# A new written order for a fused attention and two-layer kernel, with fewer changes of array division

## The chip, the core and the metric

The kernel runs on one core of a Trainium2 chip. A core has five engines, each with its own list of instructions that it takes strictly in turn: TensorE (PE), which multiplies matrices on an array of 128 by 128 cells and writes to the accumulation memory (PSUM); VectorE (DVE) and ScalarE (ACT), which work element by element and carry results out of PSUM; GpSimd (POOL) and SyncE (SP), which here mostly issue transfers (DMAs). Engines wait for one another through semaphores that the framework puts in where data or buffers pass between them. The metric is the device time of one execution in microseconds (us); less is better.

The array can be divided. A product of 128x128 uses all of it. Products of 64x64 use quarters, four of them side by side. Transposes on the array use a third division (112x64 or 128x64 here).

## The reference

Inputs are q, k and v (8 batches, 12 heads, 448 positions, 64 per head) and two weight matrices, all float32. The output is 3584 rows of 768, float32.

```python
scores = scale * np.matmul(q, k.transpose(0, 1, 3, 2))     # scale = 1/8
attn = np.maximum(scores, 0.0) ** 2 / S                    # S = 448
attn_out = np.matmul(attn, v)
x = attn_out.transpose(0, 2, 1, 3).reshape(B * S, H * D)   # 3584 x 768
h = x @ w_in                                               # 2048 wide
g = 0.5 * h * (1.0 + erf(h * inv_sqrt2))
out = g @ w_out                                            # 768 wide
```

## The kernel before

Everything is computed in bfloat16 with float32 accumulation. Heads are taken in three groups of four per batch. For batches 0 and 1, q and k are transposed on the array (`add_tq`, `add_tk`, lines 605 and 633) and copied out by ACT or DVE. For batches 2 to 7 they are transposed by transfers, nine per batch, issued by SP (`add_T_dma`, line 660; called turns below: for each group one of k and two of q).

A score piece (`add_steps`, line 734, tile `ps`) is four 64x64 products of 448 columns, one per quarter of the array, into one of three score banks (pool `w_pp`). ACT or DVE then applies the relu (lines 746 and 748) and DVE squares (line 755). After seven score pieces a group's product with v follows (`add_av`, line 795, tile `pav`, 28 products, also in a score bank), and two copies carry it to the transposed x (`xT`, lines 511 and 513). Batch 0 does all of this in halves of 224 columns.

The first layer takes, for batches 0 to 4, pieces of six 128x128 products of 448 columns (`add_f1`, line 847, tile `psh`), each followed by a gelu on ACT (line 857). Batches 5 to 7 use seven products for four blocks (`add_block`, line 991, tile `pb`) with sums on DVE. The second layer works on groups of 256 rows: group 0 plainly (`add_plain`, line 1277), groups 1 to 13 with seven products of eight matmuls each instead of eight (`add_group`, line 1166, tile `pso`). Their evictions are sums on DVE (line 1200) or copies, and SP stores the rows (line 1125).

In the last group the products are, by entry: P1407, P1409, P1411, P1413, then P1415 and P1416 (one product cut into 256 and 128 columns), P1419 (384 columns), and P1421 and P1422 (again 256 and 128). D1406 is the sum that P1421 and P1422 read. D1414 follows P1413, D1417 P1415, D1418 P1416, D1420 P1419, D1423 P1421 and D1424 P1422. S1425 to S1428 store: S1426 all 768 columns of 128 rows as a 48 KB and a 336 KB transfer, S1427 256 columns and S1428 128 columns of the other 128 rows, these two issued half by ACT and half by SP.

What comes when is written out by hand. The kernel first makes 1432 steps (`Op`), each with a function that issues its instructions. The string `ORDER` lists them all: a letter for the engine (P for PE, A for ACT, D for DVE, G for POOL, S for SP) and the step's number; Z is a filling product of zeros on PE. `place` walks through this list, `run` then calls the functions in that order, and so the order of every engine's own list, and which engine takes a relu or a copy, is what the string says:

```python
        for word in ORDER.split():
            if word[0] == "Z":
                op, eng = next(fills), "PE"
            else:
                op, eng = self.open[int(word[1:])], names[word[0]]
...
        for _, op, eng in self.log:
            op.fn(eng)
```

Since the list is complete, the costs and due times that the scheduler class also holds choose nothing; they only fill its own clock. On POOL the loads of batch b+2 stand behind gates (`add_gate`, line 701), one for each group, small copies that wait until the turns of batch b+1 have been read out of the buffers that the loads will overwrite. On SP the stores stand in one line with the turns, and a store that waits for its rows holds the turns behind it.

Before all that, PE runs warm products of zeros, 128x128 by 512 columns, while the first q and k arrive:

```python
    for _ in range(SPIN):
        nc.tensor.matmul(spin[:, 0, :], zero, zeros, start=True, stop=True)
```

Of the kernel before, what the change touches and what calls it, by code (L numbers as in the profile page):

```python
# [79 lines left out]
SPIN = 10  # L80
# [3 lines left out]
G3 G1 G0 G4 G7 G1431 G2 A10 P11 D13 A16 G6 P17 D12 P14 D18 G118 P42 P39 P21 D15 P23 G5 A43 P36  # L84
D22 P33 G117 A40 P19 D24 P25 D44 G121 A34 D20 G9 Z480 P54 P48 D41 A37 P51 D26 Z448 D38 A55 P63
P27 P29 A49 D52 P57 D28 P81 A64 D35 P69 P31 D53 G122 A58 P45 D30 D65 A82 P75 G8 D50 P131 D32 A70
P66 D59 A76 P93 D56 D46 A67 P60 D77 D47 A94 P84 P108 D71 P129 A61 G120 D68 A62 P78 D95 A109 P72
D130 D132 A79 P105 G123 D73 A85 P111 A74 D80 P96 G119 P143 D110 A106 D112 P90 D83 A97 P102 P165
D86 A144 G124 P141 A91 D166 P171 P87 A103 D98 A142 P156 D92 P133 D107 A172 P99 D104 A157 D113
P114 A88 G125 A100 D89 P135 A101 G126 A115 P168 P159 D116 G128 P174 A134 P251 A136 D169 D158  # L90
P180 A175 P145 D173 A160 A252 D181 P195 P162 P192 A146 D182 P243 D170 A193 G154 P253 D163 A196
G147 D176 A244 P198 G148 P189 D167 P186 A254 P137 D164 G151 P139 D161 A190 G150 P177 D138 A187
D140 P213 A199 P247 D178 A179 P207 P210 D214 G127 P245 A248 D200 G153 A208 P265 G149 A211 A246
P204 P216 P183 S228 P263 A205 D217 A266 P219 S229 P222 D194 P249 A264 D188 A223 S230 P257 D184
A250 D224 P259 D206 A220 D209 A258 P267 D197 D212 A260 D215 P255 D218 A268 S234 D221 P225 D185
A256 D191 S235 P201 A226 S232 P282 D227 P276 P261 A202 S233 D203 A283 P350 A262 S231 P358 A351
P348 S236 A359 P360 A277 G240 A349 G238 P354 G239 A361 P352 A355 G237 G241 P285 P288 P306 A353
P356 G155 D286 P364 G271 D307 A357 G242 G272 P318 P294 D289 P374 A365 P362 D295 A375 D319 P303
P291 D287 P279 A363 P370 D320 D278 A292 P378 A280 D304 A371 G274 D293 P309 P330 P312 D305 A379
P366 D284 D296 P372 D281 A367 P376 D313 A310 D290 G270 A331 P315 P300 G152 A373 P297 A377 D301  # L100
P368 D314 D332 A316 P333 D311 P324 P382 G269 A369 D317 G275 A334 D390 G273 D302 D419 P380 D383
D417 D418 P384 D308 A381 D393 A298 S399 D391 A325 D394 P336 S400 P387 D392 A337 A299 D338 D395
P327 P339 D385 P321 S386 A388 S398 D397 A340 P342 D396 P421 A322 S401 D328 A343 P423 D335 A422
D341 S403 P425 D323 D344 D424 P427 G407 D420 S402 D426 P429 D329 D428 S404 P443 P455 P446 D430
P433 S405 G410 D326 A444 D445 A447 P452 S406 P345 D562 A453 D456 P437 P440 D434 S436 P431 D346
A438 D347 G413 P513 G408 A441 D432 G412 P470 D457 P449 G409 P476 D442 A514 P509 G415 A450 D471
G414 P464 P479 P511 A510 G411 G416 A477 D465 P461 P494 D451 P515 A512 D448 D439 A495 P517 D454
A480 S543 P473 A462 P458 A518 A516 S541 D474 P467 P488 D481 P519 D472 S542 D560 P521 D459 A520
P523 A468 A522 P527 A489 A460 P503 A524 P500 P485 S549 A528 P525 A486 D501 P529 S546 D475 A526
D478 P497 D469 S547 P533 A530 D463 D490 P535 S435 D496 A534 S389 D466 P531 S544 A504 D498 P603  # L110
D505 P482 S548 A532 A536 D604 P491 P609 S545 P539 D561 A492 D563 P537 D502 A540 D483 P564 G556
D605 G558 A610 D499 A538 G550 D487 G557 P600 P615 D493 P566 A565 G551 D611 A601 G553 D484 G555
P612 P506 A616 G552 G554 D613 P606 P618 G559 D567 P568 D507 A508 P570 D607 A569 D608 S704 D617
P624 A619 P636 P630 P572 D620 D614 A637 D571 P574 A625 D602 D582 A631 D573 P627 P642 P651 D575
P576 A628 D643 A652 P633 D580 P639 P621 D577 S579 D626 A634 S706 D644 P666 P584 D581 S707 D632
P586 D640 A585 S578 D622 P588 A667 S705 D635 D587 D623 P590 S710 D638 D629 P663 P648 D641 S708
P645 G713 A649 D664 S711 P660 A589 P654 D665 P592 D583 A661 S709 D591 P594 D646 A655 D593 S712
D656 P657 P596 D650 D595 G716 A658 G718 D725 P676 A647 D662 G715 D668 P778 G719 D597 P769 G720
P766 A677 P678 G721 A779 D770 G714 P672 D780 A767 G717 A679 D659 P772 D653 P763 P669 A764 D773
P781 A673 P775 D765 P680 S869 A776 D782 P674 S599 D783 A681 S868 D771 P790 P682 D777 A675 D670  # L120
S598 A791 D774 P688 D768 A683 D671 P793 P787 P784 A689 S871 A788 D794 P805 P796 D792 S867 P684
D789 P686 S872 S870 G876 G878 G722 D785 A786 D806 A797 P811 D807 P802 A685 P799 P690 D798 A687
A803 D812 P692 A691 S873 D800 P694 G877 D801 A693 S875 D795 P700 D723 A695 D804 P814 P817 D724
P808 A815 D818 A701 P823 P820 D813 P698 D726 P696 D824 A699 D819 S874 P702 A697 D821 A809 P727
D825 A703 A810 P829 P912 P826 A728 P729 A830 D827 P921 A913 P924 D822 G882 P906 G883 P731 D828
A922 G879 D816 G881 D730 P733 G884 D923 D831 G880 D732 P832 D907 P918 G885 P735 D833 A919 D734
P737 A834 D908 D736 A925 D743 P933 P936 P915 D926 P739 A937 D934 D744 P942 A916 P909 P930 D738
P747 D740 S742 A910 S980 D943 P749 D917 A748 S979 P751 D931 D911 S978 D745 P948 P954 D750 P945
P753 A752 D914 S984 D746 A946 P755 D949 S983 D920 P957 P927 D950 S982 D754 D932 A958 P939 D756
P757 S985 D886 A940 D928 P759 S986 D941 A955 D938 D758 P960 P966 S761 P835 D959 S981 D760 A961  # L130
D929 P837 D887 S741 A836 D944 P839 S762 A967 D935 D947 P963 P969 D956 P951 A840 A970 D964 P972
A838 P990 D968 P843 D962 D888 A991 P841 A844 D973 P847 D952 A842 D974 A953 P845 D965 D971 A848
P987 P1002 P975 A846 A988 D1003 P993 P996 P849 D1004 A976 D992 P853 D997 A850 P859 D994 A854
D889 A977 P999 P1005 D1067 P1014 A860 P851 A1006 P855 D1015 A1000 D998 A852 D1007 P1029 P1023
D1001 P1011 A856 P857 D989 A1030 P863 D1012 A1024 D995 P1047 P1026 D1063 P1008 A864 A1048 D1027
P1041 A858 P1017 P861 D1028 A1009 D1068 A1018 D1010 P890 D1031 A862 D1059 P1053 A1042 P1020
P1050 D891 P865 D1013 A1021 D1019 P894 D1022 A1054 D1025 A1051 P1035 D1016 P1038 A866 P1032
D1060 A1039 D1043 P1044 P892 D1062 A1033 D1034 A1045 P1071 D1070 P1088 D893 P896 D1036 A1089
A895 D1049 P1073 A1072 D1179 P1090 D1069 P1079 D1040 P1092 D1055 P1096 D1074 D1052 P1077 P898
# [255 lines left out]
def kernel(  # L395
# [952 lines left out]
    zeros = zero[:, :1].to_broadcast([128, NB])  # L1348
    for _ in range(SPIN):
        nc.tensor.matmul(spin[:, 0, :], zero, zeros, start=True, stop=True)  # L1350
# [202 lines left out]
```

## Time and profile before

| | us |
|---|---|
| median of 3 runs | 371.25 (371.02 to 371.29) |
| the profiled execution's own time | 370.67 |
| its span, first to last instruction | 368.9 |
| PE busy with products | 359.5 |
| PE busy with weight loads, beside them | 218.2 |
| DVE busy | 295.6 |
| ACT busy | 187.9 |
| POOL busy | 62.6 |

The profile names a line by engine, operation and tile: `PE ps L734` is a score product, `PE psh L847` a first-layer product, `DVE a_sq L755` a square. A PE product counts as busy until its modelled end, and the products overlap, so busy time on PE is no proof that it is not waiting; the start of one product against the start of the next shows that better. The granted clock of the array is 0.998 of full pace over the span.

### The profile page before, as it was taken

The numbers are of one execution on the slowest core, as the hardware profiler recorded it, in microseconds if no ns is written. First come the engines' busy times: TensorE is split into PE (matmuls) and PEld (weight loads), VectorE is DVE, ScalarE is ACT, GpSimd is POOL, SyncE is SP. The second block draws the span as 40 slices with busy tenths as digits, with TensorE's granted clock in tenths as the row PEclk, the third lists the DMA queues.
The fourth block names the chain that finished last, engine by engine and source line by source line (L and its number), as shares of the span: only waits on it lengthen the run. The fifth ranks groups of instructions, "written<-read, shape, count | busy, mean of one in ns | idle before, by whom it ended". The sixth has DMA issues, their size and how long they took to land.

```text
span 368.9 us, 8397 instructions
## 1 busy us (share of the span) xinstructions
PE 359.5 (97%) x3532; PEld 218.2 (59%) x3532; DVE 295.6 (80%) x493; ACT 187.9 (51%) x300; POOL 62.6 (17%) x103
## 2 busy tenths in 40 slices
PE   8799999999999999999999999999999999999994
PEld 4566554455544455544555554477988778876663
DVE  3998671989884989999979998999976587677662
ACT  4999865554377565466445566861434113314200
POOL 8576206230050060022204000000000000000000
PEclk9999999999999999999999999999999999999999
DMA  9999999999989999989997994000200230022233
GB/s 171 199 201 204 201 176 157 204 201 196 191 147 188 204 129 190 211 96 196 205 145 108 205 168 133 0 2 2 87 0 3 85 87 3 12 75 85 87 86 85
DMA packets 89541, 47.26 MB, mean 128 GB/s; under 512 B 55328, under 2 KB 86048, under 8 KB 89504
## 3 DMA queue, kind: packets, MB, share of 16 engines
q0 software_dynamic: 32912, 22.47, 42.4%
q1 hardware_dynamic: 55952, 23.76, 34.4%
q8 instruction: 27, 0.44, 0.5%
q10 hardware_dynamic: 640, 0.51, 0.4%
q14 instruction: 10, 0.08, 0.1%
HBM read 45.61 MB, written 11.01 MB: 154 GB/s over the span
## 4 chain that ended last, share of the span: by engine, by line
PE 94%; DVE 3%; DMA 1%; ACT 1%; issue 0%
PE pso L1166 32%; PE psh L847 26%; PE pb L991 13%; PE ps L734 10%; PE pav L795 9%; PE pso L1277 3%; DVE a_sq L755 1%; DMA q<-in_q_dram 1%; ACT a_sq L746 1%; PE tp L605 1%; DVE qT L511 0%; PE tp L633 0%; DVE a_sq L748 0%; DVE osb L1200 0%; ACT nq L513 0%
## 5 line engine op out<-in xcount | busy, mean ns | idle before, releaser
L746 ACT ACTIVATE a_sq<-ps 128x896 bf16<-128x896 f32 (+1 forms) x114 | 100.2, 921 | 29.9 <-PE ps L734 29.7
L755 DVE TENSOR_TENSOR a_sq<-a_sq 128x896 bf16<-128x896 bf16 (+1 forms) x169 | 96.8, 615 | 1.2 <-ACT a_sq L746 0.8
L847 PE MATMUL psh<-xT,win_sb 128*128 128x448 bf16 (+1 forms) x516 | 97.3, 340 | 0.0
L748 DVE TENSOR_SCALAR a_sq<-ps 128x896 bf16<-128x896 f32 (+1 forms) x55 | 58.9, 1078 | 24.7 <-PE ps L734 24.6
L847 PEld LDWEIGHTS <-win_sb 128*128 128x128 bf16 x516 | 47.6, 98 | 46.1 <-issue 11.3
L857 ACT ACTIVATE h_sb<-psh 128x448 bf16<-128x448 f32 x80 | 43.3, 549 | 33.7 <-PE psh L847 33.5
L1166 PEld LDWEIGHTS <-s_sb 128*128 128x128 bf16 x432 | 40.7, 98 | 27.0 <-issue 3.6
L734 PE MATMUL ps<-qT,kT 64*64 64x448 bf16 (+1 forms) x756 | 48.7, 337 | 1.1 <-ACT a_sq L746 1.1
L1166 PEld LDWEIGHTS <-h_sb 128*128 128x128 bf16 x312 | 29.9, 98 | 20.2 <-issue 2.3
L1028 DVE TENSOR_TENSOR part<-pb,part 128x448 f32<-128x448 f32 x60 | 35.6, 619 | 7.4 <-PE pb L991 5.5
L1166 PE MATMUL pso<-wout_sb,h_sb 128*128 128x384 bf16 x208 | 38.1, 326 | 0.0
L1166 PE MATMUL pso<-wout_sb,s_sb 128*128 128x384 bf16 (+1 forms) x208 | 37.7, 324 | 0.1
L1166 PE MATMUL pso<-t_sb,s_sb 128*128 128x384 bf16 (+1 forms) x208 | 37.7, 324 | 0.0
L795 PE MATMUL pav<-a_sq,v_sb 64*64 64x448 bf16 (+1 forms) x756 | 36.3, 329 | 1.3 <-DVE xT L511 0.9
L734 PEld LDWEIGHTS <-kT 64*64 64x64 bf16 x756 | 18.6, 105 | 24.7 <-issue 19.9
L1200 DVE TENSOR_TENSOR osb<-pso,p_sb 128x384 f32<-128x384 f32 x39 | 21.6, 554 | 12.1 <-PE pso L1166 8.7
L1037 ACT ACTIVATE h_sb<-part 128x448 bf16<-128x448 f32 x36 | 18.6, 571 | 21.2 <-DVE part L1028 12.7
L991 PEld LDWEIGHTS <-win_sb 128*128 128x128 bf16 x288 | 27.6, 98 | 2.5 <-issue 0.4
L795 PEld LDWEIGHTS <-v_sb 64*64 64x64 bf16 x756 | 21.1, 107 | 12.6 <-issue 2.6
L701 POOL COPY gate<-qT 128x16 bf16<-128x16 bf16 x15 | 3.7, 247 | 111.5 <-DMA qT<-nq 111.5
L991 PEld LDWEIGHTS <-ws 128*128 128x128 bf16 x216 | 20.8, 98 | 1.1
L1200 DVE TENSOR_TENSOR osb<-pso,osb 128x384 f32<-128x384 f32 (+1 forms) x26 | 14.1, 544 | 7.8 <-PE pso L1166 7.5
(64 smaller groups left out, 299.8 us busy)
## 6 DMA issues: line engine op xcount, KB each, us to landing
nk<-in_k_dram POOLq DMA_DIRECT2D x23, 224.0 KB, 7.6
nq<-in_q_dram POOLq DMA_DIRECT2D x21, 224.0 KB, 7.0
v_sb<-in_v_dram POOLq DMA_DIRECT2D x5, 672.0 KB, 11.6
out_dram<-osb SPq DMA_DIRECT2D x8, 336.0 KB, 3.3
v_sb<-in_v_dram POOLq DMA_DIRECT2D x9, 224.0 KB, 8.2
out_dram<-osb SPq DMA_DIRECT2D x7, 288.0 KB, 3.2
out_dram<-osb SPq DMA_DIRECT2D x8, 240.0 KB, 3.2
win_sb<-in_moe_w_in_dram POOLq DMA_DIRECT2D x8, 192.0 KB, 9.4
```

What stands on the lines that cost most here:

```text
L734: nc.tensor.matmul(ps[64 * j : 64 * j + 64, e, x * w : x * w + w], kT[r, g, i * 128 + 64 * j : i * 128 + 64 * j + 64], moving, start=True, ...
L746: A.activation(ar, ps, AF.Relu, scale=c_att)
L748: V.tensor_scalar(ar, ps, c_att, 0.0, op0=mybir.AluOpType.mult, op1=mybir.AluOpType.max,)
L755: V.tensor_mul(box["a2"][:, :, :used], ar, ar)
L795: nc.tensor.matmul(pav[0][o2 : o2 + 64, e, :w], vt[b][r, 2 * g + e, bass.ts(i, D)], box["a2"][r, y, o : o + w], start=(i == 0), stop=(i == ...
L847: nc.tensor.matmul(ph[:, x * n : x * n + n], win_sb[:, kd, bass.ts(m + x, 128)], xT[b][:, kd, c], start=(kd == 0), stop=(kd == KD - 1),)
L857: A.activation(h_ring()[:, m : m + nm, o + c.start : o + c.stop], box[0][:, :S].rearrange("p (x n) -> p x n", x=nm), AF.Gelu,)
L991: nc.tensor.matmul(bank[name][:, y, z * HS : z * HS + HS], w[:, k, bass.ts(mm, 128)], right()[:, k], start=first and k == 0 and z == 0, st ...
L1028: V.tensor_add(get(to), ps(name), get(other))
L1037: A.activation(h_ring()[:, m : m + 2, o + half[c].start : o + half[c].stop], src().rearrange("p (x n) -> p x n", x=2), AF.Gelu,)
L1166: nc.tensor.matmul(box[bank][:, n0:n1], left()[:, kf], right()[:, kf, n0:n1], start=bool(need) and kf == 0, stop=kf == K2 - 1, skip_group_ ...
L1200: V.tensor_add(out()[:, n0:n1], box[bank][:, n0:n1], other()[:, n0:n1])
```

## The change

Two things change: the number of warm products goes from ten to nine, and the string `ORDER` is replaced. The steps are the same 1432, with two fills of zeros as before (the number behind Z is the width: the second has 480 columns instead of 448). Each engine's list is put in another order: PE's pieces, the evictions on ACT and DVE, the loads and gates on POOL, the turns and stores on SP. Some evictions also change engine: 34 relus go from ACT to DVE and 33 back, 13 copies of x go to DVE and 15 back, and of the second layer's evictions seven go to DVE and three back. In all ACT has 293 entries after 298, DVE 495 after 490. In the last group the piece of 384 columns moves ahead of the pieces of 128 and 256, and the last piece is now the one of 128 columns. The diff, cut to its first and last lines and to those with the turns and stores of batches 5 to 7:

```diff
@@ -77,89 +77,89 @@
 
 COLD_END = 0.0
 K_CUT = 4
-SPIN = 10
+SPIN = 9
 
 
 ORDER = """
-G3 G1 G0 G4 G7 G1431 G2 A10 P11 D13 A16 G6 P17 D12 P14 D18 G118 P42 P39 P21 D15 P23 G5 A43 P36
-D22 P33 G117 A40 P19 D24 P25 D44 G121 A34 D20 G9 Z480 P54 P48 D41 A37 P51 D26 Z448 D38 A55 P63
-P27 P29 A49 D52 P57 D28 P81 A64 D35 P69 P31 D53 G122 A58 P45 D30 D65 A82 P75 G8 D50 P131 D32 A70
...
-P612 P506 A616 G552 G554 D613 P606 P618 G559 D567 P568 D507 A508 P570 D607 A569 D608 S704 D617
...
-P576 A628 D643 A652 P633 D580 P639 P621 D577 S579 D626 A634 S706 D644 P666 P584 D581 S707 D632
-P586 D640 A585 S578 D622 P588 A667 S705 D635 D587 D623 P590 S710 D638 D629 P663 P648 D641 S708
...
-S598 A791 D774 P688 D768 A683 D671 P793 P787 P784 A689 S871 A788 D794 P805 P796 D792 S867 P684
...
-P747 D740 S742 A910 S980 D943 P749 D917 A748 S979 P751 D931 D911 S978 D745 P948 P954 D750 P945
...
-P1407 D1404 D1400 S1402 P1409 D1408 P1411 D1406 D1405 D1410 P1413 D1412 S1425 P1416 P1415 D1414
-D1418 P1422 D1417 P1421 D1424 S1428 P1419 D1423 S1427 D1420 S1426
+G0 G1 G4 G3 G7 G1431 G118 A10 P11 D13 P14 A16 G2 D12 P17 D15 G117 P33 P21 D18 P19 G5 P36 D22 P39
+A34 G6 P42 P25 D20 P23 G9 A37 D43 P48 D26 P51 A40 D24 P54 Z480 A49 P57 D52 P69 P27 D38 A55 P29
+P66 D35 A58 D28 G8 P75 D30 P31 P131 A70 D59 P84 D41 A76 D32 P63 D53 P129 A85 D44 P45 D56 A64
...
+G558 A565 D619 G557 P612 A616 P600 P506 A601 D613 P627 P624 P568 D507 S704 A628 D567 D508 P642
...
+D577 S579 A655 D638 P586 S709 D626 D585 P666 D635 S578 P630 P639 P588 D583 S711 D659 A631 D587
...
+A697 S598 P698 G879 D789 S873 A687 D825 P811 D804 P921 P808 D819 A699 A812 D922 P909 P814 D813
...
+A937 P747 A928 D744 D740 S742 A967 D929 P972 S980 P954 D968 P963 P749 A973 S981 A748 D964 P751
...
+D1404 D1400 S1402 P1409 D1405 D1408 P1411 D1410 P1413 D1412 S1425 P1415 D1414 P1419 D1406 D1417
+P1416 P1421 D1420 D1418 S1426 P1422 D1423 S1427 D1424 S1428
 """
```

## The prediction

> **What bounds the kernel now.** I read the page's engine shares first, then the chain in order of time, then the windows by stage, then the end.
>
> ```profile
> span 368.9 us, 8397 instructions
> ...
> PE 359.5 (97%) x3532; PEld 218.2 (59%) x3532; DVE 295.6 (80%) x493; ACT 187.9 (51%) x300; POOL 62.6 (17%) x103
> ...
> PE 94%; DVE 3%; DMA 1%; ACT 1%; issue 0%
> ```
>
> A busy PE could still wait between its pieces. The chain in order of time (start, us, what) shows that it does not:
>
> ```profile
> 65.86 0.50 PE ps L734 x8
> 66.36 2.38 PE psh L847 x12
> 68.73 0.69 PE ps L734 x12
> 69.43 2.38 PE psh L847 x12
> 71.80 0.69 PE ps L734 x12
> 72.49 3.51 PE psh L847 x18
> ...
> 106.48 1.24 PE psh L847 x6
> ```
>
> Each row begins where the one before ended, and the same mix always takes the same time. A third score piece adds 0.69 - 0.50 = 0.19 us (448 columns), so two should take 0.38; they take 0.50. A six-product piece of the first layer adds 3.51 - 2.38 = 1.13, and alone it takes 1.24. So each visit to the 64x64 division costs 0.12 + 0.11 = 0.23 us beyond its streaming. The starts in the trace split it: 0.093 us at each change of division (448 columns then take 0.282 from start to start, not 0.189), and 0.024 plus a few quadrant offsets once in a visit of two or more pieces.
>
> The windows (PE, PEld, DVE, ACT, POOL busy, with counts) show where PE does wait:
>
> ```profile
> 10.00:15.00 5.00, 4.41 (x118) 3.12 (x117) 4.99 (x11) 4.93 (x7) 2.54 (x4) 1.00 1.32 202
> 15.00:20.00 5.00, 3.41 (x106) 2.52 (x100) 4.75 (x12) 4.39 (x8) 3.34 (x6) 1.00 1.37 198
> ...
> 31.00:56.00 25.00, 25.00 (x287) 14.26 (x286) 19.19 (x31) 18.85 (x29) 5.70 (x8) 1.00 1.27 191
> ```
>
> Until 31 us VectorE and ScalarE are full and PE waits for them, 4.9 us in all by the starts in the trace (waits for a score bank, the longest 1.05 us at 17.62). From 31 us to the last group no wait but one of 0.1 us is left. The end:
>
> ```profile
> 361.63 1.03 PE L1166 MATMUL pso<-wout_sb,s_sb 128*128 128x256 bf16 x8
> ...
> 362.50 1.46 PE L1166 MATMUL pso<-t_sb,h_sb 128*128 128x384 bf16 x8
> ...
> 364.00 0.56 DVE L1200 TENSOR_TENSOR osb<-pso,p_sb 128x384 f32<-128x384 f32 x1 [0.87 <-PE pso L1166]
> ```
>
> ```profile
> out_dram<-osb SPq DMA_DIRECT2D x1, 336.0 KB, 2.8
> out_dram<-osb SPq DMA_DIRECT2D x2, 48.0 KB, 1.6
> ...
> out_dram<-osb ACTq DMA_DIRECT2D x1, 16.0 KB, 1.7
> ```
>
> The last array piece has 384 columns, its eviction takes 0.56, and the store behind it is the largest of the last group: second half issued at 364.96, landed 2.8 later (third column of these rows), and 1.1 us of closing waits follow.
>
> So the time is a start (5.75), 4.9 of opening waits, the array's own list, and the way out behind the last piece.
>
> **The change part by part.**
>
> *Divisions.* I followed the P and Z entries of both lists and marked each as 64x64 (scores, attention times v, fills), transpose, or 128x128. The old list changes division 130 times, the new one 115; the visits to 64x64 fall from 65 to 57. Pieces, products and columns are the same. 15 x 0.093 = 1.40, and 0.03 for the first pairs: **-1.43 us**, all on the path, since nothing else runs out between 31 and 360 us. By the chain's coarser rows it would be 15 x 0.115 = 1.7. A change hidden under a wait is worth nothing: of the 15, two lie before 31 us. Ends: -1.2 and -1.7.
>
> *The last group.* Taken from the start S0 of its product P1413 (358.34 before). Before: P1416, P1415, P1422, a wait of 0.23 for D1417 (`361.63`), P1421, P1419. New: P1415 at S0+1.30 (0.87 long), P1419 at 2.17 (1.30), P1416 at 3.48 (0.45), P1421 at 3.92 (0.87), P1422 at 4.79, its last product at 5.18. Its inputs, VectorE in the new order D1414, D1406, D1417, D1420, D1418 by 0.36 us from product to eviction and the spacings 0.47, 0.60, 0.34, 0.47, 0.21: D1414 ends at 2.06 (P1419 begins 0.06 later, the tightest place), D1417 at 3.0, D1418 at 4.4, all in time. The 0.23 wait goes. D1424 (0.29) ends at 5.74. SP and ACT then issue 48 and 16 KB, which land 1.6 and 1.7 later: 7.5. What is late next is the 336 KB half of S1426, issued behind D1420 at 4.85: with 2.8 it lands at 7.65. Before, the last landing was at S0+9.42. So **-1.77 us**. Ends: -1.0 (336 KB by the page's median of 3.3, and 0.3 for three stores at once) and -2.0 (the small store last).
>
> *Nine warm products.* Ten ran from 0.99 to 5.44, one per 0.43; the first transposes begin at 5.75, when ScalarE's cast of q ends (5.70). Nine end at 5.02: **0**, the cast is the cover. It cannot gain. The loss: 512 columns in 0.43 is half pace (448 take 0.19 later), and the pace has doubled by 5.75. The Trainium skill, "TensorE: Matmul & The Clock Gate", Part 1, says that a free-running window of about 3.4 us of activity opens the clock, so 0.4 us less could miss a window; the trace of before has no such miss. By the row the term is 0; by that rule, where missed, it is the third rival, and an estimate from the page's window would be +2.7 us on PE's pieces up to 8.85.
>
> *The opening.* What must be done before the first 128x128 piece, counted along the lists with the rows' spacings (ACT 0.80 a relu, DVE 1.00 a relu, 0.535 a square): VectorE 13.7 before, 13.2 new; ScalarE 14.1 and 13.6; PE's own pieces 11.75 and 11.56. That is 0.4 to 0.5 better. Before the first piece on the second half of x: VectorE 20.5 and 22.5, ScalarE 20.7 and 21.1, PE's own 19.4 and 19.6. That is 2 us more on VectorE, which had stood idle for 4 us by then (first piece 4.86, last 29.60). With the same idling PE would wait 1.7 longer; with the idle time used, nothing. Transposes moved ahead of a late cast save at most 0.2. Ends -0.5 and +1.7; **0**, because ScalarE, the fuller engine of the two in these rows, has nearly the same load.
>
> *Evictions.* 67 relus swap between ScalarE and VectorE, nearly evenly; in all ScalarE gives up five instructions, about 3 us of VectorE's 73 idle. PE's margin to its inputs after 31 us is under 0.3 us at some 15 pieces in either list: 0, ends 0 and +0.4.
>
> *Transfers.* POOL keeps 85 entries and SP 84, with the same bytes; the order differs. Scores of batches 5 to 7 come earlier on PE: by its list, batch 5 reads its transposed q and k at 153.7 instead of 158.7, batch 6 at 178.9 instead of 186.2, its group 1 at 185.2 instead of 195.9, batch 7 at 210.8 instead of 216.5. They landed 2.3 to 5.3 us ahead before, so the transfers must gain. The loop: gates wait for the last turns, then loads (seven took 132.9 to 148.3), and the first turn lands with the last load. SP's turns issue 1.3 us apart unless the queue is held:
>
> ```profile
> 180.22 7.58 SPq L660 DMA_TRANSPOSE kT<-nk  x2
> 187.85 5.62 SPq L660 DMA_TRANSPOSE qT<-nq  x2
> ```
>
> Here turns stood behind a v load issued at 179.7 (landed 191.7). New: for batch 4 a k load stands before the third gate (loads start near 101 instead of 104.4); for batch 5 the first two loads stand before the third gate (129 instead of 132.9) and store S579, which held SP until 144.4, stands behind four turns; for batch 6 the loads then start near 156 instead of 163.5, v among them, ending at 171.5. Turns of batch 6 land from 172, group 1 by 181: 6 and 4 us ahead of their readers. S742, ready at about 200, has two turns of batch 7 ahead of it, and the third lands near 204. **0**, ends 0 and +8.0 (every turn where it landed before: group 1 at 193.2 against 185.2).
>
> *Sum:* -1.43 - 1.77 = **-3.2 us**. The profiled execution took 370.67 (368.9 span and 1.8 around it), so 367.5; the median shown is 0.58 above it, which gives **368.0**.
>
> **Rivals.**
> 1. *The turns come late* (the other side). For it: PE reads batch 6 group 1 10.7 us earlier, and the old margins were 2 to 5. Against: the new queues drop the stores and the v load that held them. If the loop gains nothing: -3.2 + 8.0 = +4.8, 376.0. It decides from 4.0 us late (half of the gain needed); less leaves a gain.
> 2. *VectorE is late in the opening.* For it: 2 us more ahead of the second half. Against: its idle time. +1.7: 369.7.
> 3. *The clock opens late.* At half pace for another 4.4 us (as long as the ten products) PE's 3.1 us of pieces there would double; what the full engines after it feel is the first score piece, 0.9 to 1.5 late. Taken 1.2: 369.2. For it only the shorter run of products; against, four steady us of it remain.
>
> **How the numbers follow.** Forecast as worked out 0.76 (own range 367.0 to 369.0: the ends of divisions and last group); late turns 0.09, two thirds of it past no change; VectorE 0.10; clock 0.05. 0.2% is 0.74 us, about what a measurement here tells from no change. Faster: 0.76 + 0.10 + 0.05 and a little of the first rival, less what mixes: 0.90. Same 0.03, slower 0.07. Range 367.0 to 369.8: from the forecast's lower end to the second rival, leaving late turns out.
>
> **What would show it.** Right: the first 128x128 piece near 21.5 to 22.2 us, then a chain of PE rows without gaps; three-piece visits still 0.69; the last array piece 128 columns wide, D1424 0.29 long, the end of the span some 3.6 us behind the last array start instead of 5.2; the last landing a 336 KB store. Wrong: a row of the chain naming a DMA of qT or kT after 150 us; VectorE's xT copies ending waits near 30 us; transposes from 5.75 spaced twice as wide; or a last 336 KB store landing 3.3 us or more after its issue.

## The result, and the profile after

The changed kernel takes **381.27 us** (median of 4 executions, 377.68 to 383.0) against 371.13 before (370.5 to 371.29): a ratio of 1.027, with a 95% interval of 1.022 to 1.031. It is slower, where 368.0 was forecast. The profiled execution took 383.0 us. Ratios and intervals, here and below, leave out executions over 1.5% above the fastest of the same kernel (one of e9, one of e11, four of e16), while medians and ranges hold them all.

The page of the changed kernel: its span, PE's row, the granted clock of the array in 40 slices, and the chain's shares.

```profile
span 381.2 us, 8396 instructions
...
PE 364.2 (96%) x3531; PEld 221.0 (58%) x3531; DVE 297.9 (78%) x498; ACT 184.1 (48%) x295; POOL 64.6 (17%) x103
...
PEclk9999999999999988999998999999999999999999
...
PE 70%; DMA 10%; DVE 9%; SPq 7%; issue 2%; POOL 1%; DVEq 0%; POOLq 0%
```

Of the chain, 94% ran through PE before; now 70% does, and DMA, VectorE and SP's queue have entered it. PE's busy share alone (96%) would hide that. The digits of the clock dip at two places. The windows (PE, PEld, DVE, ACT, POOL busy with counts, granted clock, DMA share, GB/s) and PE's waits (us in total, times, longest) say where the time is:

```profile
134.00:150.00 16.00, 11.23 (x89) 5.01 (x88) 7.59 (x14) 5.34 (x7) 3.63 (x5) 0.79 1.33 161
150.00:188.00 38.00, 38.00 (x372) 19.43 (x370) 36.58 (x62) 24.61 (x36) 6.33 (x10) 1.00 1.12 176
188.00:212.00 24.00, 20.37 (x206) 10.23 (x206) 15.11 (x24) 11.51 (x17) 6.05 (x10) 0.93 0.95 136
```

```profile
PE ps L734 <- DMA kT<-nk: 8.4, 4, 4.8
```

In 134 to 150 us PE issued 89 products; the kernel before issued 165 there, by the same view of it:

```profile
134.00:150.00 16.00, 16.00 (x165) 8.66 (x156) 15.69 (x26) 8.31 (x11) 4.31 (x7) 1.00 1.27 178
```

Four score pieces wait for a turned k, the longest for 4.8 us. The chain in order of time (start, us, what) shows that wait and what follows it:

```profile
131.20 9.42 DMA kT<-nk
140.62 0.04 issue
140.66 0.96 PE ps L734 x8
141.62 2.67 PE pso L1166 x8
...
150.17 0.50 PE ps L734 x8
```

Two score pieces take 0.96 us at 140.66 and 0.50 at 150.17: behind the wait the array runs at half pace. The records of the granted clock give 0.5 from 139.92 to 146.75 (6.83 us) and from 204.77 to 208.18 (3.41 us), each beginning within a wait for kT. By the starts of the products (which give each wait about 0.2 us more than the profile's idle times do), the first wait is 4.94 us and what the half pace behind it costs is 2.9; at batch 6 the waits are 1.08, 0.69 and 2.38 us (at 188.98, 195.97 and 205.00) and the half pace there 1.5. In all that is 13.5 us.

Why that turn lands late is seen in the timeline of SP and POOL (start, us, engine, line, operation, idle time and its releaser):

```profile
130.47 0.93 POOL L701 COPY gate<-qT 128x16 bf16<-128x16 bf16 x2 [17.26 <-DMA qT<-nq]
131.20 3.20 SPq L660 DMA_TRANSPOSE kT<-nk  x2
131.44 1.42 POOL L467 DMA_DIRECT2D nq<-in_q_dram  x2
133.52 0.21 POOL L701 COPY gate<-qT 128x16 bf16<-128x16 bf16 x1 [0.66 <-DMA qT<-nq]
...
140.66 0.96 PE L734 MATMUL ps<-qT,kT 64*64 64x448 bf16 x8 [4.77 <-DMA kT<-nk]
```

Two gates open at 130.47, and two q loads of batch 5 go out at 131.44 and 132.15, ahead of the third gate. The turns of kT for groups 1 and 2 of batch 4 (S544 and S547) are issued at 131.20 and 132.93, and then land with those loads: the first at 140.62, behind the second load (139.87), although it was issued 0.2 us ahead of the first. Before, that same turn was issued at 127.17 and landed at 131.35, and the first load went out only at 132.93. The times from issue to landing of the four turns of kT between 120 and 150 us, before and after:

```profile
DMA to landing us min/median/max: 3.0/5.1/8.1
DMA to landing us min/median/max: 8.6/9.3/10.1
```

The end, in the timeline:

```profile
376.27 0.61 PE L1166 MATMUL psd<-wout_sb,s_sb 128*128 128x128 bf16 x8
...
376.91 0.29 DVE L1200 TENSOR_TENSOR osb<-psd,osb 128x128 f32<-128x128 f32 x1
376.92 0.86 ACTq L1125 DMA_DIRECT2D out_dram<-osb  x2
```

The last piece has 128 columns, as announced. From the last array start (376.66) to the end of the span are 4.57 us, against 5.22 before and 3.6 forecast.

### The profile page after: what moved, and what is told of

Read it like the earlier page. It is cut to its first block, busy times and chain, and to the rows that moved or that the text cites. A ratio compares the mean times of both kernels' runs of the same rounds, so it can differ in the third digit from the quotient of the medians.

```text
span 381.2 us, 8396 instructions
## 1 busy us (share of the span) xinstructions
PE 364.2 (96%) x3531; PEld 221.0 (58%) x3531; DVE 297.9 (78%) x498; ACT 184.1 (48%) x295; POOL 64.6 (17%) x103
## 4 chain that ended last, share of the span: by engine, by line
PE 70%; DMA 10%; DVE 9%; SPq 7%; issue 2%; POOL 1%; DVEq 0%; POOLq 0%
PE pso L1166 28%; PE psh L847 15%; PE pb L991 12%; PE ps L734 7%; DMA kT<-nk 7%; SPq L660 6%; PE pav L795 5%; DVE a_sq L755 4%; PE pso L1277 2%; DVE a_sq L748 2%; DMA nq<-in_q_dram 2%; DMA qT<-nq 1%; SPq L1125 1%; DVE ws L916 1%; POOL nq L467 1%
## 5 line engine op out<-in xcount | busy, mean ns | idle before, releaser
L746 ACT ACTIVATE a_sq<-ps 128x896 bf16<-128x896 f32 x113 | 100.2, 924 | 51.0 <-PE ps L734 50.7
L755 DVE TENSOR_TENSOR a_sq<-a_sq 128x896 bf16<-128x896 bf16 x169 | 96.4, 614 | 1.0 <-ACT a_sq L746 0.8
L734 PE MATMUL ps<-qT,kT 64*64 64x448 bf16 (+1 forms) x756 | 50.2, 349 | 10.7 <-DMA kT<-nk 8.4
L1166 PEld LDWEIGHTS <-s_sb 128*128 128x128 bf16 x432 | 41.6, 99 | 27.9 <-issue 5.2
L1166 PE MATMUL pso<-wout_sb,s_sb 128*128 128x384 bf16 (+1 forms) x208 | 39.6, 335 | 0.0
L1166 PE MATMUL pso<-wout_sb,h_sb 128*128 128x384 bf16 x208 | 39.3, 334 | 0.0
L701 POOL COPY gate<-qT 128x16 bf16<-128x16 bf16 x15 | 5.6, 373 | 102.8 <-DMA qT<-nq 102.6
L546 POOL DMA_DIRECT2D nk<-in_k_dram x23 | 16.5, 718 | 27.0 <-DMA kT<-nk 14.9
```

The source lines that it names most:

```text
L734: nc.tensor.matmul(ps[64 * j : 64 * j + 64, e, x * w : x * w + w], kT[r, g, i * 128 + 64 * j : i * 128 + 64 * j + 64], moving, start=True, ...
L746: A.activation(ar, ps, AF.Relu, scale=c_att)
L755: V.tensor_mul(box["a2"][:, :, :used], ar, ar)
L1166: nc.tensor.matmul(box[bank][:, n0:n1], left()[:, kf], right()[:, kf, n0:n1], start=bool(need) and kf == 0, stop=kf == K2 - 1, skip_group_ ...
```

## The experiments

Three theories stood against each other at first. **Theory Q**: the new order of POOL's and SP's lists is at fault. **Rival R**: the new PE list asks for turned q and k sooner than the loop of gates, loads and turns brings them, in any order. **Rival C**: the opening, where the clock came to full pace at 10.2 us and not at 5.4, sets everything behind it late. The later expectations set rival R against **theory T**: a few single entries of the two queues stand in the way, and the PE list is sound. Each run is compared with executions of the kernel before beside it (medians 370.7 to 370.9). "New" and "old" are the lists of the kernel after and before. Where lists are mixed, one planning hint of the scheduler, which issues nothing, is given a default.

### The two queues, exchanged

```diff
 after, POOL's list
-... 553 550 555 552 556 551 554 559 558 557 716 713 717 ...
+... 556 558 550 557 551 553 555 552 554 559 713 716 718 ...   (all of POOL's list old)
```

> The new kernel with POOL's list (casts, loads and gates) in the old order; SP's turns and stores, and the lists of PE, ScalarE and VectorE, stay new. Theory Q (the two transfer queues): the third gate no longer stands ahead of the next batch's loads, loads get in front of the last turns, the turns land late, PE waits and runs on at half pace for a while. With the old POOL list the wait for kT at 140 us (4.9 us and what follows it, about 7.8 in all) and the one at 205 us (2.4 and what follows, 3.9) go: 381.3 - 7.8 - 3.9 = 369.6, between 368 and 372. Rival R (the new PE list asks for the turned q and k earlier than any order of these transfers brings them): PE still waits at batches 5 and 6, some 8 us at the first place, 376 or more. Rival C (only the opening, where the fast clock comes 4.8 us later, sets everything behind it late): no change from 381.3, within 2.

Measured (e1): 384.36 us (1.038, 1.034 to 1.042). The wait at 140 us is gone. But the old POOL list also brings the opening's casts and loads in the old order, and PE's new opening doesn't fit them: a transpose waits 4.8 us for q at 36 us. A product waits 3.0 us at 161 for an output buffer (osb). The numbers of lines in this profile, and in the next and the fourth, are 3 lower.

```diff
 after
+POOL's and SP's lists, both old
```

> The new kernel with POOL's and SP's lists both in the old order; PE, ScalarE and VectorE stay new. Theory Q: 368 to 370, as in the run with POOL's list alone or up to 1 us less. Rival R: the old order landed group 1 of batch 6 at 193.2 and group 2 at 194.7, where the new PE list, unstalled, reads them at 185.2 and 191.8, so up to 8 us of waits stay: 374 to 378. Rival C: about 381. A rival S, that SP's order and not POOL's is at fault, is told apart by this run against the one with POOL's list alone: 368 to 370 here and 378 or more there.

Measured (e2): 390.97 us (1.053, 1.049 to 1.058). PE waits for turns in four places, 8.3 us in all, besides a wait of 5.3 for q at 37 us, as in e1:

```profile
PE ps L731 <- DMA qT<-nq: 8.3, 4, 2.7
```

Theory Q as it stood falls with this: the old order doesn't give the new PE list its inputs in time.

```diff
 after
-SPIN = 9
+SPIN = 10
```

> The new kernel with ten warm products in place of nine, nothing else. If nine products are why the fast clock comes at 10.2 us and not at 5.4, the first eight 112x112 transposes take 0.39 us again in place of 0.58 and the time falls by about 1.0 to 380.3; if the late opening also sets the transfers late (rival C), by far more, to 372 or less. If the clock's opening goes by something else (the gap on PE between the products and the first transposes, or chance), the first transposes stay at 0.58 and the time at 381.3.

Measured (e3): 381.6 us (1.026, 1.021 to 1.031), as the new kernel. The clock came on time (the first transposes took 0.39), and the wait for kT at 140 was there as before:

```profile
5.65 0.39 PE L633 MATMUL tp<-ident,nq 112*64 112x112 bf16 x8 [0.60 <-POOL ident L1337]
```

In the new kernel's profile that row reads 0.58. The late clock is not the doing of nine products alone either: with nine, the profiles of the runs e1, e2, e6, e9 and e13 have the clock at 4.5 to 5.8 us. In e17 below it came at 10.1 us, as in the new kernel, and that execution took 369.99 us. Rival C falls.

```diff
 before
+POOL's and SP's lists, both new
```

> The kernel before with the new lists of POOL and SP; PE, ScalarE and VectorE stay old. Theory Q: the old PE list reads kT of batch 4, group 1 at 138.2, and the new order landed it at 140.6; batch 6, group 2 at 202.9 against 205.0. So waits of 2.4 and 2.1 us, with the half pace after them 6 to 8 in all: 371.1 + 6 = 377, between 374 and 380. Rival R: the transfers are not slower, only asked for earlier: 371.1, within 1. Rival C: 371.1, within 1.

Measured (e4): 380.46 us (1.027, 1.024 to 1.031), in theory Q's range, but not in its way. No score piece waits for a turn. One product of the second layer waits, and 6.8 us at half pace follow:

```profile
PE pso L1163 <- DVE osb L1197: 4.1, 1, 4.1
```

VectorE's eviction (L1197 here) stood 5.22 us before 213.66 in front of an osb buffer, which a store frees, and that store stood in SP's queue behind turns. So the queues can cost in a second way that neither theory had: through the stores.

### The loop alone, one gate alone

```diff
 after
+POOL's list old from entry 407 (first gate of batch 3), SP's from entry 399 (first turn of batch 3)
```

> The new kernel, PE, ScalarE and VectorE new throughout, with POOL's and SP's lists new up to the turns of batch 2 (some 65 us) and in the old order from there (the loop of gates, loads, turns and stores). This is the run with both old lists without its 5 us wait for a cast in the opening, which mixed two things. Theory Q (the new order of the loop's transfers is the fault): the waits at 140 and 205 us go, 368 to 371. Rival R (the new PE list asks for batches 5 and 6 sooner than this loop turns a batch round; the old order landed the last turn of batch 5, group 0 at 155.7, batch 6 at 180.9, 193.2 and 194.7, where the new list reads at 153.7, 178.9, 185.2 and 191.8): PE ends up to 8 us late, with a half-paced stretch after the longest waits, 376 to 380.

Measured (e5): 381.38 us (1.029, 1.024 to 1.034). The opening is undisturbed now, and still five waits for turns remain, 0.9 to 2.6 us each, at 127.9, 139.8, 161.7, 200.8 and 229.1:

```profile
PE ps L734 <- DMA qT<-nq: 5.5, 4, 2.6
...
PE ps L734 <- DMA kT<-nk: 1.3, 1, 1.3
```

That is rival R's reading: lateness at every batch, with queues that served the old PE list well.

```diff
 after, POOL's list
-... G553 G550 G555 G552 G556 G551 ...
+... G553 G550 G556 G555 G552 G551 ...
```

> The new kernel with one entry of POOL's list moved: the third gate of batch 4 stands ahead of the two q loads of batch 5 and not behind them. Theory Q in its narrowest form: the turn of kT that landed at 140.6 behind those loads lands near 135, PE waits under 1 us there and keeps its full pace, 381.3 - 7 = 374. If the loop as a whole is too slow for the new list (rival R), the loads start 2.5 us later, batch 5 or 6 waits in its place, and the time is 377 or more. If that turn was late for another reason, the wait at 140 us stays, and 381.

Measured (e6): 377.31 us (1.016, 1.013 to 1.020). One entry moved takes 4.0 us off. The turn lands at 133.75 and no piece waits for a turn any more. What is late next is an eviction, for S389, which stands behind the first two turns of batch 5:

```profile
PE pso L1166 <- DVE osb L1200: 5.8, 2, 4.3
```

```profile
153.22 0.56 DVE L1200 TENSOR_TENSOR osb<-pso,p_sb 128x384 f32<-128x384 f32 x1 [4.57 <-DMA out_dram<-osb]
```

### Halves of the lists

```diff
 before
+all lists new from the 413th piece on PE
```

> The kernel before with the lists of the last 62 pieces on PE and all that belongs to them (the last group's new order and its stores) as in the new kernel; up to about 322 us nothing differs. By the prediction's term: 371.1 - 1.8 = 369.3, last array start to the end of the span 3.6 us. By what the new kernel's trace shows of its end (4.56 us against 5.22): 371.1 - 0.7 = 370.4. If the other order of pieces waits for an input, nothing or a loss.

Measured (e7): 372.04 us (1.003, 1.001 to 1.004).

```diff
 all lists new up to the 186th piece on PE, old from there
```

> All lists new up to the 186th piece on PE (about 136 us, just ahead of the scores of batch 4, group 1), all lists old from there on, with 123 changes of division in place of 130 (115 in the new kernel). By divisions alone 371.1 - 7 x 0.093 = 370.5. Rival R: the fault lies in the order after this place, 370 to 371. If the new first half leaves the transfers late (loads of batch 4 started at 107.8 against 104.4), the old rest waits for kT at 138: 373 or more.

Measured (e8): 378.66 us (1.021, 1.020 to 1.023). In these two the engines' lists were as wanted, but entries of different engines stood in another sequence in `ORDER`. The buffers of a pool are given out along that sequence, and in the second of them seven pieces waited 0.8 to 1.1 us for a PSUM bank, six of them ahead of the cut, where the new kernel has no such wait. So both were run again with the two lists simply cut at the place and joined.

> The kernel before up to its 413th piece on PE (322 us), the new kernel's lists from there, so the last group alone differs; the earlier run of this also let instructions of VectorE and ScalarE change places before the cut, and PE waited for weight sums at 309 and 318. By the prediction's term: 371.0 - 1.8 = 369.2. By the 0.67 that the end of the new kernel's trace gains: 370.3. If the order of the last pieces waits for an input: 371 or more.

Measured (e10): 371.21 us (1.001, 0.9995 to 1.002). (The cut lies at 306 us, not at 322.) The end is 0.77 shorter (below), and a wait of 1.1 us for a copy by ScalarE (tile part) at 306.9, at the seam, takes it back.

> The new kernel's lists up to the 186th piece on PE (136 us), the old ones from there, one after the other; in the earlier run of this the two were interleaved otherwise, which gave the score pieces other PSUM buffers and 8 waits for relus. By the seven changes of division saved: 371.0 - 0.65 = 370.3. With the old gates and stores from the cut on, theory T sees nothing in the way: 370 to 371. If the transfers are late out of the first half (loads of batch 4 at 107.8 against 104.4), PE waits for kT at 138: 373 or more.

Measured (e11): 373.89 us (1.006, 1.003 to 1.009), single executions from 370.24 to 377.0. The same engine lists in another sequence took 4.8 us more. The half-new kernel still has the two loads ahead of the gate, since they lie before the cut: S544 is issued at 130.04 and lands at 139.60, behind a load that lands at 139.23, and the old PE list too waits 2.07 us for it. A wait of 2.14 us for an osb buffer follows at 143.95.

> The old lists up to the 186th piece on PE (136 us), the new kernel's from there to the end: 8 changes of division fewer, the new last group. Divisions and end alone: 371.0 - 0.74 - 0.7 = 369.6. Theory T: the third gate of batch 4 is already old here, but S389 and S742 are placed as the old list (S389) and the new one (S742) have them, so 1.7 us of wait near 215: 371. Rival R: batch 6 is read too early for the loop (in the new kernel 1.1, 0.7 and 2.4 us of waits and 1.5 for half pace): 374 or more.

Measured (e12): 379.41 us (1.024, 1.020 to 1.028), the worst of what was expected. Waits for turns of batch 6 are back (0.5, 0.3 and 2.8 us), and one of 1.8 at 158.1 for a relu behind a late osb buffer; two stretches of 3.4 us at half pace follow.

### Gate and stores right, and the v loads taken out

```diff
 after, POOL's and SP's lists
-... G553 G550 G555 G552 G556 ...      -... S436 S704 S705 S389 ...   -... S978 S979 S742 S980 ...
+... G553 G550 G556 G555 G552 ...      +... S436 S389 S704 S705 ...   +... S742 S978 S979 S980 ...
```

> The new kernel with three entries moved: the third gate of batch 4 ahead of the two q loads of batch 5 on POOL (the run before had this alone: 377.3), store S389 ahead of the first turn of batch 5 on SP and store S742 ahead of the first turn of batch 7. With the gate alone no turn was waited for any more; left were 4.4 us at 153.8 and 1.7 us at 215.2, in which the second layer's product waited for VectorE's eviction, that for an osb buffer, and that for S389 and S742, which stood in SP's queue behind turns that waited for loads. Theory T (single entries of the two queues stand in the way, the PE list is sound): 377.3 - 4.4 - 1.7 (half of a 3.4 us stretch at half pace) - 1.7 = 369.5, between 368.5 and 371. Rival R (the loop turns a batch round too slowly for the new PE list): with PE no longer held at 153.8 it reads batch 5 near 153.7 and batch 6 near 179, and waits for turns again: 374 or more.

Measured (e9): 376.47 us (1.013, 1.010 to 1.017), rival R's range. Now S579 is late, and the score pieces wait because VectorE, which takes its list in turn, stands in front of an osb buffer with their relu queued behind:

```profile
157.05 0.56 DVE L1200 TENSOR_TENSOR osb<-pso,p_sb 128x384 f32<-128x384 f32 x1 [5.35 <-DMA out_dram<-osb]
...
158.66 0.59 PE L734 MATMUL ps<-qT,kT 64*64 64x448 bf16 x4 [3.58 <-DVE a_sq L748]
```

```diff
 the same, SP's list
-... S704 S705 S707 S706 S579 S709 S578 S711 ...
+... S704 S705 S579 S707 S706 S578 S709 S711 ...
```

> The run with the gate and two stores moved (376.5), with two more stores ahead: S579 behind two turns of batch 5 and not four, S578 behind four. Left in that run were 3.8 us at 158.7 (a score piece waits for a relu, VectorE stands 5.35 us before it in front of an osb buffer that S579 frees) with a half-paced stretch behind it, and 1.2 and 0.9 us for kT of batch 6. Theory T (single entries): 376.5 - 3.8 - 1.7 = 371.0. Rival R (the loop is too slow for the new PE list): PE then asks for batch 6 some 5 us sooner, the waits for kT grow by as much, 374 to 377.

Measured (e13): 375.79 us (1.012, 1.008 to 1.016), where theory T, single entries, had 371.0. The waits have moved again: 2.8 us for osb at 142.6, as the stores before S704 now land behind loads of batch 5, and 1.9 for kT of batch 6, both with 3.4 us at half pace.

```profile
PE pso L1166 <- DVE osb L1200: 2.8, 1, 2.8
PE ps L734 <- DMA kT<-nk: 1.9, 1, 1.9
```

Then the loop itself was made shorter.

```diff
 the same, and in the v load (add_v):
+            if b >= 5:
+                vt[b] = vt[4]
+                nc.gpsimd.dma_start(vx[b - 5], kv_view(v, b, 0, 1)[:, :1, :16])
+                return
             get_v(b)
             nc.gpsimd.dma_start(vt[b][:, 2 * g0 : 2 * g1], kv_view(v, b, g0, g1))
```

> The run with four stores and the gate moved, and the v loads of batches 5 to 7 left out (attention there uses v of batch 4, and a load of 4 KB stands in for each). A v load took 4.4 us of the loop. Rival R: the loop is shorter by that in batches 5 and 6, the turns land in time, and the new PE list's gain shows: 371.0 - 1.3 (divisions) - 0.7 (end) = 369. Theory T: the same 371.0 as with v, since nothing waits for the loop.

Measured (e14): **368.16 us** (368.0 to 368.59; 0.993, 0.990 to 0.995). Every wait for a turn or a store is gone, and so is the half pace (the page's clock, and the window in which the new kernel issued 89 products):

```profile
PEclk9999999999999999999999999999999999999999
```

```profile
134.00:150.00 16.00, 16.00 (x155) 8.79 (x148) 14.58 (x27) 10.19 (x13) 1.68 (x3) 1.00 1.11 166
```

> The kernel before with the v loads of batches 5 to 7 left out in the same way. Its turns landed 2.3 us and more ahead of their readers, so nothing on the path goes: 370.8, within 0.5, by theory T and by rival R.

Measured (e15): 370.67 us against 370.69 (1.000, 0.999 to 1.001). The kernel before gains nothing from the same loads taken out, so the 7.6 us between the two runs above are not the loads' own cost; they are the lateness that the new PE list feels.

> The new kernel with the v loads of batches 5 to 7 left out in the same way, nothing moved. The wait at 140 us stays, for the gate and the loads behind it are as they were (7.8 us), and the stores stay. Rival R: the waits for kT at 189, 196 and 205 us (1.1, 0.7, 2.4 and 1.5 for half pace) go: 381.3 - 5.7 = 375.6. Theory T: 380 or more.

Measured (e16): 372.3 us (368.59 to 376.42; 0.998, 0.995 to 1.001), by the median better than rival R had it. The ten executions fall apart: four lie at 375.1 to 376.4, the profiled one (375.67) among them, and six at 368.6 to 373.4. In the profiled one a single wait for a turn is left, that at 140 us, 5.0 us long; it comes from loads that were not taken out. No profile shows what the six did there.

### The v loads put elsewhere

```diff
 the run with gate and stores, S389 now behind S435, POOL's list
-... G554 G559 G558 G557 G716 G713 G717 ... G719 G722 G721 G720 G879 G885 G882 G883 ... G878 G881
+... G554 G558 G557 G716 G713 G559 G717 ... G719 G721 G720 G879 G882 G722 G883 ... G878 G881 G885
```

> The run with the gate and the stores moved (375.8), with all v loads whole, and each v load of batches 5 to 7 moved to where its stage's turns are out: that of batch 5 behind two gates of batch 5, that of batch 6 behind the gates of two groups of batch 6, that of batch 7 behind all loads of batch 7; S389 besides goes behind S435. In the run without these loads attention read v at 166.6, 196.2 and 228.4, 13 to 18 us behind the scores of the same batch. If what counts is that turns land in time (rival R): batch 5 has its turns 4.4 us sooner than with v ahead of them, batch 6 some 2 us late, since the v load of batch 5 stands ahead of its loads: 368.2 + 2 = 370.2, between 369 and 372. If the place of v is nothing and the sum of bytes alone decides: 375.

Measured (e17): 370.92 us (368.81 to 373.84) against 370.87: 1.001, 0.998 to 1.003. Its profiled execution took 369.99 us and has no wait for a turn, and one of 0.4 us for v at 168.6.

```diff
 the same, but G559 stays between G554 and G558
```

> The same, with the v load of batch 5 left among the loads of batch 5, where it was; those of batches 6 and 7 moved as above. Rival R: batch 6 is relieved and batch 5 not; turns of batch 5, group 0 landed at 155.7 to 156.6 against a reader at 153.4, so some 2.5 us of waits near 155, with a half-paced stretch of 1.7 if they are over 2 us: 368.2 + 2.5 to 4.2 = 371 to 372.5. If the bytes alone decide: 375.

Measured (e18): 370.51 us (368.06 to 373.47): 1.000, 0.998 to 1.002. Its profiled execution took 368.3 us and has no wait for a turn at all, at batch 5 neither, against the expectation. So with a gate, four stores and two or three v loads put elsewhere the new order stands level with the old one, and single executions reach the forecast; the 5 us between its executions remain. Rival R falls in its strict form, "in any order": in the profiled execution of e18 the loop serves this PE list in time with every load whole. What is left of it is that the margin is thin, and of theory T that more entries stood in the way than the gate and the stores. S389 moved together with the v loads in these two runs, so its part in them isn't told apart. No version with all its loads beat the kernel before clear of the noise.

## Why the prediction was wrong, point by point

**Transfers, 0 (ends 0 and +8.0): this step failed.** Between the new kernel (381.27) and the one with gate, stores and v loads out of the way (368.16) lie 13.1 us. Gate and four stores give 5.5 of them (to 375.79), the v loads the other 7.6. Taken in the other order the shares differ: the v loads alone give 9.0 (to 372.3 in e16), gate and stores the other 4.1. So the parts can't be priced one by one. The working went wrong in three sentences:

- "for batch 5 the first two loads stand before the third gate (129 instead of 132.9)" was booked as a gain for the loads. What those loads run beside, the last two turns of kT of batch 4, was not asked, though the prediction itself says that "the first turn lands with the last load". It cost 4.0 us by the run that moves the gate alone.
- "store S579, which held SP until 144.4, stands behind four turns" was booked as a gain for SP. Who waits for the store was not asked: it frees an osb buffer, VectorE waits for that, and its relus stand behind.
- "They landed 2.3 to 5.3 us ahead before, so the transfers must gain." They didn't. Loads of batch 6 started at 170.0 where 156 was worked out (163.5 before), and its first turn landed at 186.3 where 172 was (175.5 before).

A figure that would have warned of it was in the trace of before, unread. There the last turn of group 0 landed at 123.5, 155.7 and 180.9 in batches 4, 5 and 6: two rounds of the loop took 57.4 us. The old PE list read that group's first scores at 125.8, 158.7 and 186.2, 60.4 us from first to last; the new one, with nothing in its way, reads them at 125.1, 153.4 and 178.6 (in the run without the v loads), 53.5 us. That is 3.9 less than the loop took, with 2.3 in hand at batch 4. Without the v loads those turns landed at 122.6, 151.1 and 176.2: two rounds in 53.6 us. That the loads and not the reader set the old pace is borne out by e15, where the old PE list has the same turns at 124.6, 153.8 and 179.4, 54.8 us. It is no fixed bound: in e18, with two of the v loads put elsewhere, the two rounds took 54.7 us.

**The first rival, turns late, 0.09, 376.0.** It was the right mechanism with too small a chance and a price too low by 5 us. The place was not batch 6 but first batch 4, and the price assumed that each turn landed where it had before; under the new queues the last kT of batch 6 landed at 204.96, 11 us later than before. And it had no term for the half pace behind a long wait, which made up 4.4 of the 13.5 us.

**Divisions, -1.43: right.** In the run without v loads (e14) and the kernel before without them (e15), PE takes 356.0 us and 357.9 from the first array piece to the last start. Added up from the starts after 31 us, what the changes between 64x64 and 128x128 cost beyond the streaming is 8.59 us in e14 (92 changes) and 10.04 in e15 (106): 1.45 us less, at 0.093 for nearly every change in both (448 columns take 0.282 across one and 0.189 otherwise). The rest of the 1.87 lies in the opening and, with 0.12, in the last group.

**The last group, -1.77 (ends -1.0 and -2.0): mis-sized.** From the start of P1413 to the end of the span it takes 10.53 us before and 9.75 in the new kernel: -0.77, outside both ends. PE did what was worked out, to 0.01 us (P1419 at 2.17, the last start at 5.18). The stores did not. The 336 KB one took 2.9 us, where 2.8 was put. The small ones behind it were priced at 1.6 and 1.7 us from rows where few others were under way; issued within 0.5 us of each other and next to the 336 KB, they took 2.6 to 2.8, and the last landing is a 16 KB store at 8.53 and not the large one at 7.65.

**Nine products, 0: right** for the median (ten give 381.6). In the profiled execution the clock did open late, as the third rival had it: the transposes were spaced twice as wide (0.048 us and not 0.025), and the first 128x128 piece began at 22.92 us, 0.75 later than before. But this comes and goes between kernels with nine (10.2 us here, 10.1 in e17, 3.7 to 5.8 in ten others, of which three fell back to half pace once more before 9 us). **The opening, 0, and evictions, 0: right.** By the starts the waits until 30 us come to some 4 to 5 us in the kernels that keep the new opening, as they do before; the second rival's 1.7 us didn't come.

Put together, what the new lists for PE, VectorE and ScalarE are worth where no transfer is late is 2.5 us (368.16 against 370.69 of the kernel before beside it), of the 3.2 expected; the end is 1.0 short of its term. That 368.16 lies so near the forecast of 368.0 is in part luck, since the forecast started from 371.25. The lists that were forecast as covered, POOL's and SP's, were the ones that decided.

## What to carry to other kernels

When one engine's list gets shorter at some place, read the period of the loop that feeds it (start of a batch's loads to start of the next) before counting the gain: here a margin of 2.3 us at one batch was used up when the reader's two rounds (53.5 us) fell below the loop's (57.4). When an entry moves in a queue, ask both what it passes and who waits for what it passes; here a load let in before the last turns had landed, and a store put behind turns that waited for loads, cost more than the moved entries saved.

## What the runs showed of the hardware that was not expected

**A turn that runs beside loads lands with them.** From the starts and landings of transfers in the traces:

```
kernel                 turn   issued   last load beside it     turn lands
new                    S542   115.53   124.32 (v)              124.72
new                    S544   131.20   139.87 (q)              140.62
new                    S868   176.82   185.94 (k)              186.26
new                    S873   195.91   204.66 (v)              204.96
new second half        S873   192.33   201.64 (v)              201.94
without v loads        S704   140.26   143.65 (k)              144.62
```

A turn with nothing beside it takes some 3 to 4 us from issue to landing (S544 before: 4.2), one beside loads up to 9.4. The loads needn't be first: those beside S544 were issued 0.24 and 0.95 us behind it. The single packets in the trace of the new kernel show how. Turns move in packets of 256 bytes on SP's queue, 896 to a turn here. From 131.5 to 132.5 us, with no load under way, 344 and 324 of them start in each half microsecond; from 133.0 to 134.5, beside 66 to 84 packets of the loads, only 21 to 79, and the last of S544 and S547 start after 141. The Trainium skill, "DMA: Bandwidth & Descriptors", section "Queues, rings and completion order", says that a transfer's completion is a strongly ordered write, which lands only after every earlier write of that DMA engine, across its queues. The landings in the table agree with that, but by the packets the data itself came late here, so no run shows that this rule held a turn back.

**Half pace after waits shorter than expected.** In the records of the granted clock every stretch but the last, which the end cuts off, is a multiple of 3.41 us (1 for 3.41, 2 for 6.83, 38 for 129.71, 106 for 361.81). Cut into windows of that length, the traces of all runs show for the windows at full pace from 12 us to the last group: where PE idled 2.16 us or more of a window, half pace followed each time (13 windows); at 1.92 to 1.98 us it followed four times of six; at 1.80 or less never. So the place of a wait counts beside its length. The wait of 1.84 us in e12 lay whole in one window and brought half pace; those of 2.07 and 2.14 (e11) and 2.56 (e3) were split between two windows and did not. Half pace lasted a second window where the wait reached 0.7 us or more into the first. (PE's idle time goes by the profile's modelled ends.) The Trainium skill, "TensorE: Matmul & The Clock Gate", "Why this matters for your kernels", asks for no idle gap over about 3 us; by these runs a gap of 1.8 can be enough. Its Part 1 has a free-running window, and these records agree with that.

**Spread as a sign of a used-up margin.** The kernel before varied by about 1 us between most executions, and the new lists without v loads by 0.6 (four executions of e14). Several kernels whose turns land just in time or late varied by 5 to 8 (the new kernel: 377.68 to 383.0; e16: 368.59 to 376.42; e18: 368.06 to 373.47). In two executions the same transfers of batch 3 and 4 landed 1.5 to 4 us apart (S542 at 123.41 in e13 and 119.55 in e14, ahead of anything that differs). Where that comes from stayed open.
